# `P*V` on four 32-column tiles, shared scores behind the row sums: an attention and two-layer MoE kernel on one Trainium2 core

## The chip, the cores and the metric

The kernel runs on one core of a Trainium2 chip. The metric is the device time of one execution in microseconds (us). TensorE is called PE here, its weight loads PEld, VectorE DVE, ScalarE ACT, GpSimd POOL and SyncE SP, as in the profile.

## The reference

Attention with a soft cap over 2 batches of 12 heads, 448 rows, head size 64; its output feeds two feed-forward stages with gates.

```python
def _attn_ref(q, k, v, cap):
    scale = 1.0 / np.sqrt(q.shape[-1])
    scores = scale * np.matmul(q, k.transpose(0, 1, 3, 2))
    scores = cap * np.tanh(scores / cap)
    scores = scores - np.max(scores, axis=-1, keepdims=True)
    attn = np.exp(scores)
    attn = attn / (np.sum(attn, axis=-1, keepdims=True) + 1e-09)
    return np.matmul(attn, v)
...
def reference(**kwargs):
    ...
    x = np.ascontiguousarray(attn_out.transpose(0, 2, 1, 3)).reshape(B * S, H * D)
    x = _moe_ref(x=x, **moe_kwargs)      # h = x @ w_in; h * sigmoid(1.702 h) @ w_out
    return _moe2_ref(x=x, **moe2_kwargs) # rms norm, silu(x @ w_gate) * (x @ w_val) @ w_out
```

## The kernel before

The program has two parts, one behind the other: `attention()`, which works on the 24 heads as 12 pairs (p = 0 to 11), and `rest()`, the feed-forward stages, a long row of matrix products with weights that ACT and DVE decode on the way. The order of the work is written out by hand, in the loop over p at the end of `attention()`; each engine takes its instructions in the order in which this loop issues them. So an instruction that has to wait holds up all that stands behind it on its engine.

For a pair, PE turns q and k (`turn`, 64-row pieces), DVE splits them into a high and a low part (`split_kq`), and PE makes the transposed scores in four pieces of up to 128 keys: pieces 0 to 2 for both heads of the pair (`scores`, two 64-row tiles of the array side by side, into a two-bank tile `s`), and the last 64 keys of both heads together in one (`scores_last`, the full 128 x 128 array, into a one-bank tile `v`). These last are the shared scores. ACT takes tanh and exp of each piece (`exps`, tiles `tt` and, for the shared scores, `tl`). PE multiplies the result by v (`outputs`, `P*V`: the two heads on two 64-column tiles of the array side by side, in four rounds, one for each piece) and sums the rows (`sums`: four 32-column tiles side by side, in two rounds when DVE has added up the first three pieces, which it does for the pairs in `THIRD`, and in three for pairs 6 to 9). DVE copies `P*V` out (`zt`), takes the reciprocal of the sums, and POOL writes it to DRAM (`keep_recips`) and reads it back spread over all rows (`spread`, `r<-recs`); then come `norm_mul` (DVE), `norm_hi` (POOL, ACT for the last pairs) and `norm_lo` (DVE), which give the feed-forward part its x.

`P*V` and the sums of pair p-1 stand in the loop's pass p, behind the first scores of pair p+1. Tiles come from pools in PSUM: two buffers for `s` (`ps_s`), two for `v` (`ps_v`, which shared scores, `P*V` and sums share), one for `t`. A tile can be written only when what stood in its buffer has been read:

```python
ps_s = actx.enter_context(tc.tile_pool(name="ps_s", bufs=2, space=PSUM, reuse_waits="tile"))
ps_t = actx.enter_context(tc.tile_pool(name="ps_t", bufs=1, space=PSUM, reuse_waits="tile"))
ps_v = actx.enter_context(tc.tile_pool(name="ps_v", bufs=2, space=PSUM, reuse_waits="tile"))
```

Of the kernel before, what the change touches and what calls it, by code (L numbers as in the profile page):

```python
# [10 lines left out]
F32R = mybir.dt.float32r  # L11
# [7 lines left out]
def attn_moe_kernel(  # L19
# [14 lines left out]
    nc = tc.nc  # L34
# [8 lines left out]
    NC = 3  # L43
# [5 lines left out]
    def f(ap):  # L49
        return ap.bitcast(F32)  # L50
# [143 lines left out]
    def attention():  # L194
        with ExitStack() as actx:
# [14 lines left out]

            vns = [ap_.tile([128, 4, NC, D], F32, name=f"vn{i}", bufs=1) for i in range(3)]
            ves = [ap_.tile([128, 2, 2, D], F32, name=f"ve{i}", bufs=1) for i in range(3)]
            kbs = [ap_.tile([128, 2, 128], F32R, name=f"kb{i}", bufs=1) for i in range(2)]

            def constants():
                for kb in kbs:
# [71 lines left out]
            def split_kq(p):  # L288
                t = turned.pop(p)
                if p:  # L290
                    x = ap_.tile([128, 2, 2 * S], F32R, tag="x", name="x")
                    xs[p] = [[x[:, a, j * S:(j + 1) * S] for j in range(2)] for a in range(2)]
                    flat = t[:, :, 0:S].rearrange("p a (c n) -> p a c n", n=64)
                    high, low = [x[:, m].rearrange("p (c a n) -> p a c n", a=2, n=64) for m in range(2)]
                    nc.vector.tensor_copy(high, flat)
                    nc.vector.tensor_tensor(out=low, in0=flat, in1=f(high), op=ALU.subtract)  # L296
                    for e in range(2):
                        nc.gpsimd.tensor_copy(kbs[p % 2][half[e], :, half[e]], f(x[half[e], :, 384:S]))  # L298
                else:
                    ts = [t[1][:, 0:128], t[1][:, 128:S], t[0][:, 64:64 + S]]  # L300
                    xs[p] = [
                        [ap_.tile([128, w.shape[1]], F32R, name=f"x{a}{j}", bufs=1) for j, w in enumerate(ts)]
                        for a in range(2)
                    ]
                    for j in (2, 0, 1):
                        nc.scalar.activation(out=xs[p][0][j], in_=ts[j], func=AF.Copy)
                    for j in (2, 0, 1):
                        nc.vector.tensor_tensor(out=xs[p][1][j], in0=ts[j], in1=f(xs[p][0][j]), op=ALU.subtract)
                    for a in range(2):
                        for e in range(2):  # L310
                            nc.gpsimd.tensor_copy(kbs[0][half[e], a, half[e]], f(xs[p][a][1][half[e], 256:S - 128]))
# [16 lines left out]
            def scores_last(p):  # L328

                ps = ps_v.tile([128, 512], F32, tag="v", name="v")  # L330
                for n, (a, m) in enumerate(TERMS):
                    nc.tensor.matmul(  # L332
                        out=ps[:, 0:S], lhsT=kbs[p % 2][:, a], rhs=xs[p][m][-1], start=(n == 0), stop=(n == 2)
                    )
                return ps

            def exps(p, c, ps):
                if c == NC:
                    t = ap_.tile([128, S], F32, tag="tl", name="tl")
                    src_ = ps[:, 0:S]  # L340
                else:
                    t = ap_.tile([128, 2, S], F32, tag="tt", name="tt", bufs=8)
                    src_ = ps[:, :, 0:S]
                nc.scalar.activation(out=t, in_=src_, func=AF.Tanh, scale=tsc)  # L344
                nc.scalar.activation(out=t, in_=t, func=AF.Exp, scale=capt)  # L345
                pt[p, c] = t
# [4 lines left out]
            def outputs(p, cs=range(NC + 1)):  # L351

                g, i = place[p]
                if 0 in cs:
                    opened[p] = ps_v.tile([128, 512], F32, tag="v", name="v")
                ps = opened[p]
                for c in cs:
                    for e in range(2):
                        w = vns[g % 3][:, 2 * i + e, c] if c < NC else ves[g % 3][:, i, e]
                        nc.tensor.matmul(  # L360
                            out=ps[half[e], 0:S], lhsT=w, rhs=pt[p, c][:, e] if c < NC else pt[p, c],
                            start=(c == 0), stop=(c == NC), skip_group_check=True,
                        )
                if NC not in cs:
                    return
                zt[p] = zrp.tile([128, S], F32, tag="z", name="z", bufs=5)
                if p < NPR - 1:
                    nc.vector.tensor_copy(zt[p], ps[:, 0:S])
                else:
                    nc.scalar.activation(out=zt[p], in_=ps[:, 0:S], func=AF.Copy)  # L370
# [96 lines left out]
            def warm_up(times):  # L467
# [3 lines left out]
            warm_up(WARM)  # L471

            plan_a = {
                5: [(size, 0)], 7: [(size, 1)], 10: [(high_part, 0)],
                12: [(high_part, 1), (square, 2), (sign, 2), (mask, 2)], 13: [(square, 3), (sign, 3), (mask, 3)],
            }
            plan_d = {
                6: [(clip, 0), (field, 0)], 7: [(top, 0)], 8: [(low, 0)], 9: [(clip, 1), (field, 1)],
                10: [(top, 1), (low, 1)],
            }  # L480

            def decode(plan, p):
# [10 lines left out]
            turn(0)  # L493
            split_kq(0)
            s0 = scores(0, 0)
            for p in range(NPR + 1):
                if p < NPR:
                    exps(p, 0, s0)
                    if p != 1:
                        s1 = scores(p, 1)  # L500
                    exps(p, 1, s1)
                    s2 = scores(p, 2)
                    decode(plan_a, p)
                    exps(p, 2, s2)
                    last = scores_last(p)
                    exps(p, NC, last)
                    if p == 0:
                        turn(1)
                        split_kq(1)
                        outputs(0, range(2))  # L510
                        s0 = scores(1, 0)
                    if p + 2 < NPR:
                        turn(p + 2)
                        split_kq(p + 2)
                    for g, at_ in ((2, 0), (3, 0), (4, 1), (5, 3), (6, 5)):
                        if p == at_:
                            load_k(g)
                            load_q(g)
                    if p in (1, 2, 4, 5, 7):
                        load_v(2 + (1, 2, 4, 5, 7).index(p))  # L520
                    if p in (2, 4, 6):
                        load_to((2, 4, 6).index(p))
                    if 0 < p < NPR - 1:
                        s0 = scores(p + 1, 0)
                    if p == 0:
                        s1 = scores(1, 1)
                    if p != 1:
                        add_two(p)
                    if p == NPR - 2:
                        run(low_part, 0)  # L530
                else:
                    decode(plan_a, p)
                    run(low_part, 1)
                if p == 0:
                    outputs(0, range(2, NC + 1))
                elif p == 2:
                    outputs(1, range(2, NC + 1))
                elif p > 2:
                    outputs(p - 1)
                if 4 <= p < NPR:  # L540
                    norm_mul(p - 4)
                if p == NPR - 1:
                    both = ps_t.tile([128, 2, 512], F32, tag="t", name="late")
                    for n in range(2):
                        late[p - 2 + n] = both[:, :, n * SH:(n + 1) * SH]
                    spread_product(p - 2, [late[p - 2][:, j] for j in range(2)])
                if 3 <= p < NPR:
                    spread(p - 3)
                if p >= 1:
                    sums(p - 1)  # L550
                if 4 <= p < NPR:
                    norm_hi(p - 4)
                if 1 <= p < NPR - 2:
                    keep_recips(p - 1)
                if p == 1:
                    add_two(1)
                if p in THIRD:
                    add_third(p)
                if 4 <= p < NPR:
                    norm_lo(p - 4)  # L560
                if p == 1:
                    outputs(1, range(2))
                if p == NPR - 1:
                    normal(p - 2)
                if p == NPR:
                    spread_product(p - 2, [late[p - 2][:, j] for j in range(2)])
                    normal(p - 2, p - 4)
                    decode(plan_a, p + 1)
                decode(plan_d, p)
            return spread_product, norm_mul, norm_hi, norm_lo  # L570

    def rest(spread_product, norm_mul, norm_hi, norm_lo):
# [371 lines left out]
```

## Time and profile before

| | |
|---|---|
| timed runs | 603.66, 603.69, 604.91 us, median 603.69 |
| profiled execution | 607.85 us |
| its span, first to last instruction | 606.1 us |
| PE busy | 597.0 us (99% of the span) |
| ACT busy | 396.2 us (65%) |
| DVE busy | 454.0 us (75%) |

The attention part ends on PE at 107.31 us, where the first product of the feed-forward part starts. A matmul of this kernel is a group of records: an x12 row is twelve matmul records in sequence or side by side. Ends of matmuls are modelled, so lengths of PE's work are read from the start of one row to the start of the next.

### The profile page before, as it was taken

The page shows a single profiled execution, that of the slowest core. Times are in us where ns is not written, and L with a number is a line of the kernel's source. Part 1 is how long each engine was busy: PE and PEld are TensorE (multiplying, and loading weights), DVE is VectorE, ACT ScalarE, POOL GpSimd, SP SyncE. Part 2 cuts the span into 40 slices and gives each one's busy share as a digit, 9 for nine tenths or more (in the row PEclk, how much of TensorE's full clock was granted, in tenths as well). Part 3 has the DMA queues.
Part 4 walks back from the last instruction along what each step waited for, and adds up shares of the span by engine and source line. Part 5 has one row for each costly group of instructions (what it writes and reads, how often), then busy time and mean ns, then how long its engine had stood idle before and what let it go on. Part 6 is the DMA issues. An engine that isn't in the chain of part 4 may idle for free.

```text
span 606.1 us, 8596 instructions
## 1 busy us (share of the span) xinstructions
PE 597.0 (99%) x3389; PEld 506.4 (84%) x3389; DVE 454.0 (75%) x549; ACT 396.2 (65%) x532; POOL 76.9 (13%) x105
## 2 busy tenths in 40 slices
PE   8999899999999999999999999999999999999997
PEld 5455454889988899888888888899989999999997
DVE  2888799689874636667788899995588897588842
ACT  5999967789874547777676666674555483366400
POOL 4233441000000000000022203200022200122100
PEclk9999999999999999999999999999999999999999
DMA  6666422064453332333333333433233342233012
GB/s 152 157 182 170 127 76 91 1 184 135 152 157 104 105 104 73 120 122 105 104 105 107 101 105 107 136 123 104 62 120 122 114 132 86 97 104 105 0 79 104
DMA packets 78567, 67.16 MB, mean 111 GB/s; under 512 B 29440, under 2 KB 75830, under 8 KB 78528
## 3 DMA queue, kind: packets, MB, share of 16 engines
q1 hardware_dynamic: 74064, 64.27, 34.7%
q0 software_dynamic: 3664, 2.16, 1.2%
q8 instruction: 26, 0.43, 0.3%
q10 hardware_dynamic: 800, 0.20, 0.1%
q14 instruction: 13, 0.11, 0.1%
HBM read 63.80 MB, written 2.78 MB: 110 GB/s over the span
## 4 chain that ended last, share of the span: by engine, by line
PE 91%; DMA 3%; ACT 3%; DVE 2%; POOL 0%; issue 0%; POOLq 0%; DVEq 0%
PE b L630 22%; PE b L629 22%; PE b L628 22%; PE b L838 14%; PE v L360 4%; DMA r<-recs 3%; PE s L322 2%; PE v L393 1%; ACT tt L345 1%; ACT tt L344 1%; PE v L332 1%; PE v L469 1%; DVE rs L398 1%; POOL kb L298 0%; PE t L274 0%; DVE x L296 0%
## 5 line engine op out<-in xcount | busy, mean ns | idle before, releaser
L630 PE MATMUL b<-x,ring 128*128 128x512 f32 (+1 forms) x480 | 174.3, 363 | 0.0
L629 PE MATMUL b<-x,ring 128*128 128x512 f32 (+1 forms) x480 | 174.1, 363 | 0.0
L628 PE MATMUL b<-x,ring 128*128 128x512 f32 (+1 forms) x480 | 174.0, 362 | 0.0
L628 PEld LDWEIGHTS b<-x,ring 128*128 128x128 f32 x480 | 90.1, 188 | 10.4 <-issue 0.3
L629 PEld LDWEIGHTS b<-x,ring 128*128 128x128 f32 x480 | 90.1, 188 | 9.9
L630 PEld LDWEIGHTS b<-x,ring 128*128 128x128 f32 x480 | 90.1, 188 | 9.4
L838 PE MATMUL b<-ring,uA 128*128 128x384 f32 x504 | 87.8, 334 | 0.0
L838 PEld LDWEIGHTS b<-ring,uA 128*128 128x128 f32 x504 | 87.4, 188 | 0.0
L154 DVE SCALAR_TENSOR_TENSOR dec<-raw,dec 128x768 uint32<-128x768 uint32 x66 | 67.8, 1028 | 24.7 <-ACT dec L150 23.3
L160 DVE SCALAR_TENSOR_TENSOR dec<-raw,dec 128x768 uint32<-128x768 uint32 x68 | 73.2, 1077 | 1.1
L180 DVE TENSOR_TENSOR ring<-dec,ring 128x768 fp32r<-128x768 f32 x68 | 66.8, 984 | 4.7 <-ACT ring L175 4.6
L630 PE MATMUL b<-g,ring 128*128 128x384 f32 (+1 forms) x192 | 70.0, 365 | 0.0
L629 PE MATMUL b<-g,ring 128*128 128x384 f32 (+1 forms) x192 | 69.8, 364 | 0.0
L175 ACT ACTIVATE ring<-dec 128x768 fp32r<-128x768 f32 x68 | 56.7, 834 | 19.9 <-DVE dec L166 11.7
L628 PE MATMUL b<-g,ring 128*128 128x384 f32 (+1 forms) x192 | 69.6, 362 | 0.0
L166 DVE SCALAR_TENSOR_TENSOR dec<-raw,dec 128x768 uint32<-128x768 uint32 x68 | 65.0, 955 | 1.5
L146 ACT ACTIVATE dec<-dec,edge 128x768 f32<-128x768 f32 x66 | 61.6, 933 | 1.0
L142 ACT ACTIVATE dec<-raw 128x768 f32<-128x768 f32 x66 | 59.1, 896 | 0.8 <-DVE ring L180 0.5
L150 ACT ACTIVATE dec<-dec 128x768 f32<-128x768 f32 x66 | 55.6, 843 | 1.5
L806 POOL TENSOR_TENSOR a<-a,gg 128x512 f32<-128x512 f32 (+1 forms) x18 | 29.6, 1646 | 188.6 <-DVE gg L799 184.2
L809 ACT ACTIVATE uA<-a 128x512 fp32r<-128x512 f32 (+1 forms) x24 | 13.9, 579 | 46.3 <-POOL a L806 34.5
L730 POOL TENSOR_TENSOR sqs<-sqs,sq 128x384 f32<-128x384 f32 (+1 forms) x10 | 11.7, 1166 | 229.7 <-ACT sq L726 229.7
(107 smaller groups left out, 697.0 us busy)
## 6 DMA issues: line engine op xcount, KB each, us to landing
raw<-in_moe_w_out SPq DMA_DIRECT2D x20, 768.0 KB, 4.2
raw<-in_moe_w_in SPq DMA_DIRECT2D x16, 768.0 KB, 4.6
raw<-in_moe_w_gate SPq DMA_DIRECT2D x12, 768.0 KB, 4.2
raw<-in_moe_w_val SPq DMA_DIRECT2D x12, 768.0 KB, 4.3
raw<-in_moe_w_out SPq DMA_DIRECT2D x8, 512.0 KB, 3.7
out<-oacc SPq DMA_DIRECT2D x6, 384.0 KB, 2.3
raw<-in_moe_w_out SPq DMA_DIRECT2D x8, 256.0 KB, 3.4
r<-recs POOLq DMA_DIRECT2D x9, 224.0 KB, 7.7
```

The costliest lines, as they stand in the source:

```text
L142: nc.scalar.activation(out=f(d), in_=f(hi), func=AF.Square, scale=2.0 ** 15)
L146: nc.scalar.activation(out=f(d), in_=f(d), func=AF.Sign, bias=edge)
L150: nc.scalar.activation(out=f(d), in_=f(d), func=AF.Relu, scale=2.0 - 2.0 ** -23)
L154: nc.vector.scalar_tensor_tensor(out=d, in0=hi, scalar=3, in1=d, op0=ALU.logical_shift_left, op1=ALU.bitwise_and)
L160: nc.vector.scalar_tensor_tensor(out=d, in0=hi, scalar=0xC0000000, in1=d, op0=ALU.bitwise_and, op1=ALU.bitwise_or)
L166: nc.vector.scalar_tensor_tensor(out=d, in0=lo, scalar=29, in1=d, op0=ALU.logical_shift_right, op1=ALU.bitwise_or)
L175: nc.scalar.activation(out=t[:, 0], in_=f(dec_t[w][0]), func=AF.Copy)
L180: nc.vector.tensor_tensor(out=t[:, 1], in0=f(d), in1=f(t[:, 0]), op=ALU.subtract)
L628: nc.tensor.matmul(out=wide(o, b), lhsT=w0, rhs=x0, start=first, stop=False)
L629: nc.tensor.matmul(out=wide(o, b), lhsT=w0, rhs=x1, start=False, stop=False)
L630: nc.tensor.matmul(out=wide(o, b), lhsT=w1, rhs=x0, start=False, stop=last)
L838: nc.tensor.matmul(out=os_[t][n][:, 0:HW], lhsT=uA[xi][:, i, tok], rhs=w[:, wi, n * HW:(n + 1) * HW], start=(i == 0 and xi == 0 and wi == ...
```

## The change

Four things are changed. `P*V` of a pair runs on four 32-column tiles (two halves of each head) in place of two of 64 columns; the number of rounds stays four. The shared scores of pair p, and their tanh and exp, move from the front of pass p to behind the sums of pair p-1, except in the first and the last pass; for this `kb` and `x` get a third buffer, and the exps of the next pair's first piece go ahead of those of the shared scores. `spread` is issued at the front of POOL's part of a pass, ahead of the casts, and `norm_mul` stands behind the reciprocal, `norm_lo` a pass later. Two of the weight steps of the first units (`high_part`, `low_part` of unit 1) move into the last passes.

```diff
-            kbs = [ap_.tile([128, 2, 128], F32R, name=f"kb{i}", bufs=1) for i in range(2)]
+            kbs = [ap_.tile([128, 2, 128], F32R, name=f"kb{i}", bufs=1) for i in range(3)]
...
-                    x = ap_.tile([128, 2, 2 * S], F32R, tag="x", name="x")
+                    x = ap_.tile([128, 2, 2 * S], F32R, tag="x", name="x", bufs=3)
...
                 for c in cs:
-                    for e in range(2):
+                    for n in range(4):
+                        e, d0 = n // 2, n % 2 * 32
                         w = vns[g % 3][:, 2 * i + e, c] if c < NC else ves[g % 3][:, i, e]
                         nc.tensor.matmul(
-                            out=ps[half[e], 0:S], lhsT=w, rhs=pt[p, c][:, e] if c < NC else pt[p, c],
+                            out=ps[32 * n:32 * n + 32, 0:S], lhsT=w[:, d0:d0 + 32],
+                            rhs=pt[p, c][:, e] if c < NC else pt[p, c],
                             start=(c == 0), stop=(c == NC), skip_group_check=True,
                         )
...
-                5: [(size, 0)], 7: [(size, 1)], 10: [(high_part, 0)],
-                12: [(high_part, 1), (square, 2), (sign, 2), (mask, 2)], 13: [(square, 3), (sign, 3), (mask, 3)],
+                5: [(size, 0)], 7: [(size, 1)], 9: [(high_part, 0)], 11: [(high_part, 1)],
+                12: [(square, 2), (sign, 2), (mask, 2)], 13: [(square, 3), (sign, 3), (mask, 3)],
...
-                10: [(top, 1), (low, 1)],
+                10: [(top, 1), (low, 1)], 11: [(low_part, 1)],
...
+            exps(0, 0, s0)
             for p in range(NPR + 1):
+                early = p in (0, NPR - 1)
                 if p < NPR:
-                    exps(p, 0, s0)
                     if p != 1:
                         s1 = scores(p, 1)
                     exps(p, 1, s1)
                     s2 = scores(p, 2)
-                    decode(plan_a, p)
                     exps(p, 2, s2)
-                    last = scores_last(p)
-                    exps(p, NC, last)
+                    if early:
+                        last = scores_last(p)
+                        exps(p, NC, last)
+                        decode(plan_a, p)
+                    if p >= 3:
+                        spread(p - 3)
...
                     if 0 < p < NPR - 1:
                         s0 = scores(p + 1, 0)
+                    if p < NPR - 1:
+                        exps(p + 1, 0, s0)
...
+                    if p >= 5:
+                        norm_lo(p - 5)
...
                 elif p > 2:
                     outputs(p - 1)
-                if 4 <= p < NPR:
-                    norm_mul(p - 4)
+                if p in THIRD and p != 1:
+                    add_third(p)
+                if p < NPR - 2:
+                    decode(plan_d, p)
...
-                if 3 <= p < NPR:
-                    spread(p - 3)
                 if p >= 1:
                     sums(p - 1)
...
-                if p in THIRD:
-                    add_third(p)
...
                 if 4 <= p < NPR:
-                    norm_lo(p - 4)
+                    norm_mul(p - 4)
+                    norm_hi(p - 4)
+                if not early and p < NPR:
+                    last = scores_last(p)
+                    decode(plan_a, p)
+                    exps(p, NC, last)
```

On PE, before, in the pass of pair 3: two pieces of scores (`s_481`, `s_491`), the shared scores `v_501`, the transposes `t_508`, the next pair's first piece `s_536`, and `P*V` into `v_545`.

```order
L322 MATMUL s_481<-x_350 128x448 [waits PE_49]
L322 MATMUL s_481<-x_350 128x448 x5
L322 MATMUL s_491<-x_350 128x448 [waits Activation_49]
L322 MATMUL s_491<-x_350 128x448 x5
L332 MATMUL v_501<-x_350,kb1_111 128x448 [waits DVE_49,Pool_49]
L332 MATMUL v_501<-x_350,kb1_111 128x448 x2
L274 MATMUL t_508<-ident_58,kq1_103 128x64 x14
L322 MATMUL s_536<-x_439 128x448 [waits Activation_49]
L322 MATMUL s_536<-x_439 128x448 x5
L360 MATMUL v_545<-tt_394,vn1_105 64x448 [waits DVE_49]
```

The same place of the change, from the shared scores of pair 2 (`v_492`) to `P*V` of pair 2 (`v_561`):

```order
L332 MATMUL v_492<-x_281,kb2_112 128x448 [waits DVE_49,Pool_49]
L332 MATMUL v_492<-x_281,kb2_112 128x448 x2
L322 MATMUL s_499<-x_353 128x448 [waits Activation_49]
L322 MATMUL s_499<-x_353 128x448 x5
L322 MATMUL s_509<-x_353 128x448 [waits Activation_49]
L322 MATMUL s_509<-x_353 128x448 x5
L274 MATMUL t_521<-ident_58,kq1_103 128x64 x14
L322 MATMUL s_549<-x_446 128x448 [waits Activation_49]
L322 MATMUL s_549<-x_446 128x448 x5
L361 MATMUL v_561<-tt_376,vn1_105 32x448 x4
```

The shared scores are now the last thing of a pass, one pass's work ahead of the `P*V` that needs them (its fourth round reads `tl_496`); the first piece `s_549` takes the buffer that `s_499` had.

On ACT, in the change, the same stretch: what reads `s_456` (first piece of pair 3), `v_492` (shared scores of pair 2), then `s_499` and `s_509`.

```order
L344 ACTIVATE tt_463<-s_456,tsc_60 128x896 [waits PE_49]
L345 ACTIVATE tt_463<-tt_463,capt_59 128x896 [waits Activation_49]
L344 ACTIVATE tl_496<-v_492,tsc_60 128x448 [waits PE_49]
L345 ACTIVATE tl_496<-tl_496,capt_59 128x448 [waits Activation_49]
L344 ACTIVATE tt_506<-s_499,tsc_60 128x896 [waits DVE_49,PE_49]
L345 ACTIVATE tt_506<-tt_506,capt_59 128x896 [waits Activation_49]
```

Here the tanh of `s_499` (which frees the buffer for `s_549`) stands behind tanh and exp of the shared scores; before, it stood ahead of those of its own pair.

On POOL, one pass in the middle, before (casts for `kb`, the spread, `norm_hi`, the reciprocals to DRAM):

```order
L298 CAST kb0_110<-x_813 64x2x64 x2
L408 DMA r_841<-recs_662 128x1x448
L435 CAST x0_66<-z_554 128x448
L403 DMA recs_855<-rs_852 4x224
L298 CAST kb1_111<-x_907 64x2x64 x2
```

and in the change:

```order
L410 DMA r_832<-recs_691 128x1x448
L298 CAST kb2_112<-x_849 64x2x64 x2
L405 DMA recs_901<-rs_899 4x224
L437 CAST x0_66<-z_578 128x448
L410 DMA r_932<-recs_799 128x1x448
```

The spread now goes out right behind the `norm_hi` of the pass before, ahead of the casts, which wait for the split.

## Rows read from the trace of the kernel before

**Rows 1.** The page's first line.

```profile
span 606.1 us, 8596 instructions
```

**Rows 2.** Busy time of each engine in two stretches (columns as in the first line).

```profile
core 0: us, PE busy (x) PEld busy (x) DVE busy (x) ACT busy (x) POOL busy (x), PEclk, DMA share, GB/s
...
107.30:606.00 498.70, 495.35 (x2536) 453.26 (x2532) 369.94 (x451) 306.04 (x428) 41.28 (x28) 1.00 0.33 106
```

**Rows 3.** PE in order of time, one pair: start, length, operation, count.

```profile
41.67 2.48 PE L360 MATMUL v<-tt,vn 128*64 128x448 f32 x12
43.97 0.92 PE L360 MATMUL v<-tl,ve 128*64 128x448 f32 x4
44.82 0.59 PE L393 MATMUL v<-ts,ones 128*32 128x224 f32 x8
45.23 0.56 PE L393 MATMUL v<-tl,blk 128*32 128x224 f32 x8
45.72 1.49 PE L322 MATMUL s<-x 64*128 64x448 f32 x12
47.13 0.88 PE L332 MATMUL v<-x,kb 128*128 128x448 f32 x3
47.95 0.65 PE L274 MATMUL t<-ident,kq 64*128 64x64 f32 x14
48.40 0.85 PE L322 MATMUL s<-x 64*128 64x448 f32 x6
49.19 2.48 PE L360 MATMUL v<-tt,vn 128*64 128x448 f32 x12
```

**Rows 4.** ACT in order of time, one pair, and a weight step between pairs.

```profile
36.18 0.62 ACT L344 ACTIVATE tl<-v,tsc 128x448 f32<-128x448 f32 x1
36.83 0.67 ACT L345 ACTIVATE tl<-tl,capt 128x448 f32<-128x448 f32 x1
37.40 0.99 ACT L344 ACTIVATE tt<-s,tsc 128x896 f32<-128x896 f32 x1
...
43.32 0.61 ACT L344 ACTIVATE tl<-v,tsc 128x448 f32<-128x448 f32 x1
...
48.63 0.89 ACT L128 ACTIVATE dec<-raw 128x768 f32<-128x768 f32 x1
```

**Rows 5.** PE in order of time, `P*V` of pair 6; in brackets the wait ahead.

```profile
74.33 3.78 PE L360 MATMUL v<-tt,vn 128*64 128x448 f32 x12 [2.12 <-DVE rs L398]
77.88 1.37 PE L360 MATMUL v<-tl,ve 128*64 128x448 f32 x4
```

**Rows 6.** DVE in order of time, `norm_mul` ahead of that wait.

```profile
72.18 0.62 DVE L423 TENSOR_TENSOR z<-z,r 128x448 f32<-128x448 f32 x1 [3.18 <-DMA r<-recs]
```

**Rows 7.** What the view of line L408 (`spread`) says of its nine transfers.

```profile
DMA to landing us min/median/max: 6.8/7.7/10.4
```

**Rows 8.** Busy time and granted clock of two stretches behind that wait.

```profile
74.30:75.30 1.00, 0.97 (x6) 0.49 (x8) 1.00 (x2) 1.00 (x2) 0.55 (x1) 1.00 0.16 58
75.30:78.70 3.40, 3.40 (x13) 0.98 (x8) 3.37 (x4) 1.58 (x2) 0.82 (x1) 0.51 0.01 1
```

**Rows 9.** PE and ACT in order of time, where one waited for the other.

```profile
8.77 1.01 ACT L344 ACTIVATE tt<-s,tsc 128x896 f32<-128x896 f32 x1 [0.89 <-PE s L322]
9.83 0.88 PE L322 MATMUL s<-x,x 64*128 64x448 f32 x6 [0.50 <-ACT tt L344]
...
80.45 1.49 PE L322 MATMUL s<-x 64*128 64x448 f32 x12
81.37 1.01 ACT L344 ACTIVATE tt<-s,tsc 128x896 f32<-128x896 f32 x1 [4.46 <-PE s L322]
```

**Rows 10.** PE in order of time, row sums in three rounds (pair 8).

```profile
87.49 0.56 PE L393 MATMUL v<-tt,ones 128*32 128x224 f32 x8
87.87 0.56 PE L393 MATMUL v<-tl,blk 128*32 128x224 f32 x8
```

**Rows 11.** DVE and PE in order of time, first reciprocal and `P*V` of pair 1.

```profile
22.35 1.55 DVE L398 RECIPROCAL rs<-v 128x224 f32<-128x224 f32 x1
...
22.51 1.72 PE L360 MATMUL v<-tt,vn 128*64 128x448 f32 x8 [0.93 <-ACT tl L344]
```

More of the change, by code (lines that the diff above doesn't have):

```diff
@@ L297, in split_kq @@
                     for e in range(2):
-                        nc.gpsimd.tensor_copy(kbs[p % 2][half[e], :, half[e]], f(x[half[e], :, 384:S]))
+                        nc.gpsimd.tensor_copy(kbs[p % 3][half[e], :, half[e]], f(x[half[e], :, 384:S]))
                 else:
@@ L332, in scores_last @@
                     nc.tensor.matmul(
-                        out=ps[:, 0:S], lhsT=kbs[p % 2][:, a], rhs=xs[p][m][-1], start=(n == 0), stop=(n == 2)
+                        out=ps[:, 0:S], lhsT=kbs[p % 3][:, a], rhs=xs[p][m][-1], start=(n == 0), stop=(n == 2)
                     )
@@ L530, in attention @@
                         run(low_part, 0)
+                    if p >= 5:
+                        norm_lo(p - 5)
                 else:
                     decode(plan_a, p)
-                    run(low_part, 1)
+                    norm_lo(p - 5)
                 if p == 0:
@@ L546, in attention @@
                     spread_product(p - 2, [late[p - 2][:, j] for j in range(2)])
-                if 3 <= p < NPR:
-                    spread(p - 3)
                 if p >= 1:
                     sums(p - 1)
-                if 4 <= p < NPR:
-                    norm_hi(p - 4)
                 if 1 <= p < NPR - 2:
@@ L556, in attention @@
                     add_two(1)
-                if p in THIRD:
-                    add_third(p)
+                    add_third(1)
                 if 4 <= p < NPR:
-                    norm_lo(p - 4)
+                    norm_mul(p - 4)
[4 more added lines that the diff above has]
+                    exps(p, NC, last)
                 if p == 1:
                     outputs(1, range(2))
+                if NPR - 2 <= p < NPR:
+                    decode(plan_d, p)
                 if p == NPR - 1:
@@ L568, in attention @@
                     decode(plan_a, p + 1)
-                decode(plan_d, p)
             return spread_product, norm_mul, norm_hi, norm_lo
```

## The prediction, written before the changed kernel ran

> **What bounds the kernel now.** I read the busy times by stretch first. From 107.3 us on the feed-forward part takes 498.70 us of the span of 606.1, and PE works in 495.35 of it [rows 1, 2]: PE is the bound there, the change adds no work to it, and what the attention part gains or loses ahead of it goes to the end one for one. So I read PE's own order of time next. In the middle of the attention part one pair follows the next without a wait: from `P*V` at 41.67 to `P*V` at 49.19 are 7.52 us, all of it PE's work [rows 3]. The reader sees there `P*V` (2.30 for three rounds, 0.85 for the fourth), the sums (0.41 and 0.49), two pieces of scores (1.41), the shared scores (0.82), the transposes (0.45), the next first piece (0.79). ACT needs 7.14 for a pair (36.18 to 43.32) [rows 4], so it is nearly as full, 0.38 below PE.
>
> Then I looked for breaks. There is one that matters: ahead of `P*V` of pair 6 PE waited 2.12 us for the reciprocal, and then `P*V` took 3.78 and 1.37 [rows 5] where it takes 2.48 and 0.92 [rows 3]. The granted clock shows why: 0.51, the lower of its two levels (1.2 GHz in place of 2.4), in the 3.4 us from 75.3 on, after that wait [rows 8]. The wait begins on DVE: `norm_mul` stood 3.18 us for the spread reciprocals [rows 6], whose transfer needed 10.4 us, the longest of nine (median 7.7) [rows 7], and the reciprocal that PE needs stands behind it. Wait and low clock cost 2.12 + 1.75 = 3.87 us (1.75 is 3.78 + 1.37 less 2.48 + 0.92).
>
> **The spread and its use.** The transfer is now issued ahead of the casts, and its reader stands behind the reciprocal. Before, it had 10.4 - 3.18 = 7.2 us from issue to use. Now it goes out right behind the `norm_hi` of one pass and is read behind the reciprocal two passes later: two passes of 7.5 less reciprocal, `norm_mul`, cast and issue, some 3 us, leave about 12. The longest landing, 10.4, fits. So 3.87 us go; should a transfer be late all the same, it holds `norm_mul` and no longer the reciprocal. Term: -3.87, or 0 where the wait isn't there to begin with (below).
>
> **`P*V` on four tiles.** Rounds stay four, and a round has the same 448 columns. The sums show four 32-column tiles side by side: 0.38 for 224 columns (87.49 to 87.87) [rows 10], which is 0.76 for 448, against 0.77 for a round on two tiles of 64 (2.30 / 3) [rows 3]. So a round costs the same. What goes is the change of shape between `P*V` and sums: the fourth round takes 0.85 in place of 0.77, the first sum 0.41 in place of 0.38 [rows 3, 10], together 0.11 a pair.
>
> The Trainium skill ("TensorE: Matmul & The Clock Gate", section "Measured speedup vs the span model") speaks against such packing: it gives three column tiles side by side a speed-up of 2.38, which is 79% of three. By that, as an estimate, `P*V` would take 3.07 / 0.79 = 3.9 us a pair, 0.8 more, some 9 us for eleven pairs. The sums' rounds above, at 0.76 for 448 columns, don't show this loss.
>
> **The shared scores behind the sums.** This is the part that decides, and I think that it costs more than it gives. On PE alone it saves a shape change, about 0.1 a pair. But it closes a loop through ACT. The shared scores now end a pass; ACT takes their tanh and exp, and only then the tanh of the next pair's second piece; that one frees the buffer which the first piece of the pair after it needs (it waits for ACT in the order shown above); and behind that piece stand `P*V`, sums and the next shared scores. One turn of the loop:
> shared scores to ACT's start 0.92 (80.45 to 81.37, where ACT did wait for PE) [rows 9]; tanh 0.65 and exp 0.57 (36.18, 36.83, 37.40) [rows 4]; tanh of the second piece until PE goes on 1.06 (8.77 to 9.83, where PE did wait for ACT) [rows 9]; first piece 0.79; `P*V` 3.15 - 0.08 = 3.07; sums 0.38 + 0.49 = 0.87 [rows 3].
> Sum 7.93 us, where the pass took 7.52: +0.41. With a third round of sums both grow by 0.38 [rows 10]. A shape change from 32 columns to the full array stands nowhere in the trace; I take it as that from sums to scores, inside the 0.49. Bounds: without any handover above streaming the loop can't come below the 7.52 less 0.2 that PE itself needs; 8.1 if DVE's copy of `P*V`, which must now be done before the shared scores can take its buffer, comes 0.15 late.
> The loop holds in seven passes (from the second pieces of pair 4 to those of pair 11): 7 x 0.41 = 2.9. In the last of them the transposes (0.45) are missing; this shortens PE's own sum and not the loop: +0.4. Term: +3.3, from +1 to +4.5.
> ACT has 7.93 - 7.14 = 0.79 of room in a turn; the weight steps put ahead of the shared exps (0.89) [rows 4] overrun it once, in pass 5: +0.1. In passes 7 and 9 the third round of sums covers them.
>
> **The head.** The first reciprocal runs from 22.35 to 23.90, and DVE's order up to it is unchanged. `P*V` of pair 1 began at 22.51, when the tanh of its shared scores had freed a buffer [rows 11]. Now it takes the buffer of the sums, which this reciprocal reads: start 23.96. Behind it stand 1.7 of `P*V`, then scores and handover 0.92: ACT restarts at 26.6, takes three pieces of 1.97 ((7.14 - 1.22) / 3) until 32.5, and from the shared exps the loop runs on: + 7.93 - 0.92 to the shared scores of pair 3, + 0.82 to the next pieces, 40.3. Before they began at 45.72 - 7.52 = 38.2. Term: +2.1.
> PE waits here about 2 us, as long as the wait behind which the clock fell. There the fall came 1.0 us after work resumed [rows 5, 8]; here it would catch some 1.2 us of work on the path and cost as much. Bounds 0 and 1.2; I take 0.4, because a fall that comes a little later finds ACT at work and costs nothing.
>
> **The rest.** Two shape changes fewer at the end: -0.2. `norm_lo` a pass later, the third buffers and their memset lie beside PE's work. `high_part` and `low_part` of unit 1 leave the stretch behind the last exps, where ACT and DVE decode the next units while PE starts the feed-forward part; PE doesn't wait there now (495.35 busy, and its chain unbroken), and with less in front of them the later units come no later. Without that cover each 0.8 us of ACT would show.
>
> **Sum**, against the profiled 607.85 (span 606.1 and 1.75 around it): 2.1 + 3.3 + 0.1 + 0.4 - 3.87 - 0.2 = +1.8, so 609.7. The median of the timed runs, 603.69, is 4.16 below the profiled time; carried over, 605.5 us.
>
> **Rivals.**
> *The wait was never in the timed runs.* 4.16 is close to the 3.87 of wait and low clock; a transfer that lands 3 us earlier leaves neither. Two timed runs 0.03 apart speak for it, the third, 1.2 higher, for a wait that comes and goes. Then nothing is won back: 605.5 + 3.9 = 609.4. Chance 0.26.
> *The loop doesn't bind* (the faster side). If the handovers through ACT were 0.41 shorter in all, PE would run on its own work, 7.52 - 0.2: seven passes give -1.5, and with +2.1, -3.87 and -0.2 the time is 600.2. It decides from a loop of 7.52 down. Against it: of 0.92 and 1.06 about 0.57 and 0.99 are streaming itself, so all of what is left would have to vanish. Chance 0.15.
> *A loop somewhat short.* 7.85 in place of 7.93, no fall of the clock and a head of +1.8: 605.5 - 0.6 - 0.4 - 0.3 = 604.2, not to be told from before. Chance 0.27.
> *The four tiles share a path.* If they ran two by two, a round would take twice 0.77: +3 us a pair, over 630 us. The sums speak against it. Chance 0.02; this is the mechanism of the skill's 2.38 above, in its extreme.
>
> **How the numbers follow.** The sum as it stands has 0.30: 605.5 us, and with the other cases the range is 602.2 to 609.2, which leaves out most of the faster rival and the upper part of the first. About 0.2%, 1.2 us, is what a measurement of this kernel can tell from no change. Slower: 0.30 + 0.26 + 0.02 = 0.58. Same: 0.27. Faster: 0.15.
>
> **What would show it.** Right: in every middle pass a wait of PE of about 0.6 us ahead of the first piece (`scores`), released by ACT's tanh; a pass of 7.9 and 8.3 us; ACT waiting up to 0.8 for the shared scores; no wait of the reciprocal for the transfer; a wait of some 2 us for DVE's reciprocal ahead of `P*V` of pair 1; rounds of `P*V` at 0.76. Wrong: passes of 7.3 without a wait; or rounds above 0.8; or waits for decoded weights behind 108 us, which the sum leaves out.

## The result, and the profile after

The changed kernel takes 608.33 us (median of 6 runs, 608.11 to 610.46), the kernel before, beside it, 604.13 us (6 runs, 603.66 to 604.91). The ratio is 1.0078, with a 95% interval from 1.0065 to 1.0090: slower by 0.8%, which is 4.7 us (the medians lie 4.2 apart). That lies inside the forecast range and on the forecast side, but 2.8 us above the 605.5 given as likeliest. It is near the first rival's 609.4, that the wait had never been in the timed runs.

The profiled executions alone would say something else: 608.16 us after against 607.85 before, nearly the same. So the first question is which of the two is a typical execution. Of the changed kernel, the page's first line, two stretches of busy time with the granted clock (PEclk), and PE in order of time: `P*V` of pair 1, then one pair of the middle.

```profile
span 606.4 us, 8970 instructions
```

```profile
23.20:27.50 4.30, 4.24 (x48) 2.53 (x48) 2.62 (x3) 2.86 (x4) 0.62 (x1) 1.00 0.85 192
...
107.96:606.40 498.44, 495.01 (x2536) 453.07 (x2532) 369.64 (x451) 305.50 (x427) 41.35 (x28) 1.00 0.33 106
```

```profile
23.19 1.71 PE L361 MATMUL v<-tt,vn 128*32 128x448 f32 x16 [1.82 <-DVE rs L400]
...
38.83 0.85 PE L332 MATMUL v<-x,kb 128*128 128x448 f32 x3
39.61 1.49 PE L322 MATMUL s<-x 64*128 64x448 f32 x12
40.93 0.59 PE L274 MATMUL t<-ident,kq 64*128 64x64 f32 x14
42.00 0.87 PE L322 MATMUL s<-x 64*128 64x448 f32 x6 [0.47 <-ACT tt L344]
42.80 2.46 PE L361 MATMUL v<-tt,vn 128*32 128x448 f32 x24
45.08 0.94 PE L361 MATMUL v<-tl,ve 128*32 128x448 f32 x8
45.83 0.56 PE L395 MATMUL v<-ts,ones 128*32 128x224 f32 x8
46.21 0.56 PE L395 MATMUL v<-tl,blk 128*32 128x224 f32 x8
46.85 0.85 PE L332 MATMUL v<-x,kb 128*128 128x448 f32 x3
...
70.68 0.56 PE L395 MATMUL v<-tl,blk 128*32 128x224 f32 x8
71.17 0.87 PE L332 MATMUL v<-x,kb 128*128 128x448 f32 x3
```

From shared scores to shared scores a pass now takes 46.85 - 38.83 = 8.02 us, where it took 7.52 [rows 3], and PE stands still in it, ahead of the first piece of the next pair, for ACT's tanh. In the whole attention part such waits sum up to 4.8 us in nine places, 0.47 in most; the one of 0.50 right behind the first scores stands before the change too [rows 9], so 4.3 us in eight places are new. ACT and DVE in the same pass, in order of time, and the first reciprocal:

```profile
39.72 0.64 ACT L344 ACTIVATE tl<-v,tsc 128x448 f32<-128x448 f32 x1 [0.81 <-PE v L332]
40.38 0.67 ACT L345 ACTIVATE tl<-tl,capt 128x448 f32<-128x448 f32 x1
40.96 0.99 ACT L344 ACTIVATE tt<-s,tsc 128x896 f32<-128x896 f32 x1
```

```profile
21.59 1.55 DVE L400 RECIPROCAL rs<-v 128x224 f32<-128x224 f32 x1
...
46.08 0.62 DVE L370 COPY z<-v 128x448 f32<-128x448 f32 x1 [1.23 <-PE v L361]
```

The reader sees the ring close: PE waits for ACT's tanh of 40.96, that stands behind the exps of the shared scores, and ACT had waited 0.81 for PE's shared scores of 38.83. Neither engine is full (7.46 of 8.02 us for PE), and both wait in each pass. Of transfers of the reciprocals nothing is waited for; the view of `spread`'s line (L410) says

```profile
DMA to landing us min/median/max: 6.8/8.1/9.4
```

### The profile page after: what moved, and what is told of

It reads as the page before. It is cut to its first block, busy times and chain, and to the rows that moved or that the text cites. A ratio compares the mean times of both kernels' runs of the same rounds, so it can differ in the third digit from the quotient of the medians.

```text
span 606.4 us, 8970 instructions
## 1 busy us (share of the span) xinstructions
PE 592.8 (98%) x3581; PEld 506.1 (83%) x3581; DVE 454.7 (75%) x549; ACT 396.8 (65%) x532; POOL 79.8 (13%) x106
## 3 DMA queue, kind: packets, MB, share of 16 engines
q0 software_dynamic: 3664, 2.16, 1.3%
## 4 chain that ended last, share of the span: by engine, by line
PE 92%; ACT 4%; DVE 2%; issue 1%; DMA 1%; SPq 0%
PE b L643 22%; PE b L642 22%; PE b L641 22%; PE b L851 14%; PE v L361 5%; ACT tt L344 2%; PE s L322 2%; PE v L395 1%; PE v L332 1%; ACT tl L344 1%; ACT tt L345 1%; DVE x L296 1%; DVE x L295 1%; DMA kq<-in_k 1%; ACT tl L345 0%
## 5 line engine op out<-in xcount | busy, mean ns | idle before, releaser
L641 PEld LDWEIGHTS b<-x,ring 128*128 128x128 f32 x480 | 90.1, 188 | 10.4 <-issue 0.3
```

Of the source, the lines that this page charges most:

```text
L641: nc.tensor.matmul(out=wide(o, b), lhsT=w0, rhs=x0, start=first, stop=False)
```

## The experiments

My theory after the result: the wait of before belongs to single executions, so nothing was won back; late head and loop through ACT are the whole loss. Rivals: the wait is in the timed runs too and the change loses some 8 us elsewhere; or the four tiles or DVE set the longer pass.

The last column is the attention part in the profiled execution, from PE's first scores to the first product of the feed-forward part (both starts in brackets). It leaves out the start of the program, which varies by itself (last section).

| kernel | median us | ratio to before, 95% | attention us |
|---|---|---|---|
| before, profile shown ahead | 603.69 | | 99.71 (7.60, 107.31) |
| changed | 608.33 | 1.0078, 1.0065 to 1.0090 | 101.17 (6.79, 107.96) |
| b_again | 603.60 | 1.0000, 0.9992 to 1.0009 | 95.87 (6.85, 102.72) |
| spread_only | 603.94 | 1.0003, 0.9994 to 1.0012 | 96.62 (6.84, 103.46) |
| four_only | 603.70 | 1.0002, 0.9992 to 1.0012 | 96.69 (7.76, 104.45) |
| early_all | 602.64 | 0.9976, 0.9965 to 0.9986 | 94.97 (7.45, 102.42) |
| head_only | 606.68 | 1.0054, 1.0042 to 1.0067 | 99.68 (7.59, 107.27) |
| exp_later | 605.23 | 1.0033, 1.0022 to 1.0044 | 98.07 (6.76, 104.83) |
| exp_later_head | 603.72 | 1.0002, 0.9993 to 1.0012 | 96.44 (7.44, 103.88) |
| pad_loop | 614.68 | 1.0185, 1.0167 to 1.0204 | 106.66 (6.75, 113.41) |

The first four experiments ran beside 35 runs of before (median 603.93), the last four beside 17 (603.22); they are compared by their ratios.

**b_again: before once more, unchanged.**

> The kernel before, unchanged, for a second profile and more times. Theory A (the wait for the late reciprocals belongs to the one profiled execution and not to the timed ones): no wait of PE ahead of P*V of pair 6, no stretch at the lower clock in the attention part, feed-forward part about 3.9 us earlier than 107.31, so about 103.4, span about 602.2, time 603.7 to 604.2. Theory B (every execution has it, and the timed ones are shorter elsewhere): again a wait of about 2 us and the lower clock behind it, span about 606.

The page's first line, PE at the `P*V` that had waited, and the line on `spread`'s transfers. (The texts ahead call it that of pair 6. It is pair 7's: the sums behind it are the second with three rounds, and pairs 6 to 9 have three.)

```profile
span 601.5 us, 8596 instructions
```

```profile
70.65 0.86 PE L322 MATMUL s<-x 64*128 64x448 f32 x6
71.44 2.48 PE L360 MATMUL v<-tt,vn 128*64 128x448 f32 x12
73.74 0.92 PE L360 MATMUL v<-tl,ve 128*64 128x448 f32 x4
```

```profile
DMA to landing us min/median/max: 6.8/7.4/9.1
```

No wait, and `P*V` takes 2.30 and 0.85 (starts 71.44, 73.74, sums at 74.59). Where [rows 5] show 2.12 of waiting and [rows 8] the lower clock, there is nothing; the longest landing is 9.1 in place of 10.4 [rows 7]. The attention part is 3.84 us shorter, which is the 3.87 of the prediction. Theory A holds: the profile that the prediction was read from was a rare execution: at 607.85 it lies above all 35 timed runs of before in this comparison, the highest of which took 605.76. The granted clock says the same: its mean over the span was 0.997 in that execution, and 0.999 or 1.000 in each of these 35, in the ten of b_again and in the 17 beside the later experiments.

**spread_only: the moves around `spread` alone, on the kernel before.**

```diff
                     exps(p, NC, last)
+                    if p >= 3:
+                        spread(p - 3)
...
-                if 4 <= p < NPR:
-                    norm_mul(p - 4)
...
-                if 3 <= p < NPR:
-                    spread(p - 3)
                 if p >= 1:
                     sums(p - 1)
...
+                if 4 <= p < NPR:
+                    norm_mul(p - 4)
+                    norm_hi(p - 4)
```

(`norm_lo` goes a pass later, as in the change.)

> The kernel before with nothing but the moves around the spread: issued ahead of the casts, used behind the reciprocal, norm_lo a pass later. Theory A (the timed runs of before have no such wait): within 0.5 us of before. Theory B (the wait is in them): 3 to 4 us faster.

Ratio 1.0003: nothing was won in the median. Its runs lie closer together, 603.56 to 604.40, against 603.09 to 605.76 of before. The profile has no wait for a transfer, but one new wait of PE, for DVE's copy of `P*V`, which DVE now reaches later near the end:

```profile
98.88 2.48 PE L360 MATMUL v<-tt,vn 128*64 128x448 f32 x12 [0.69 <-DVE z L368]
```

**four_only: `P*V` on four tiles alone, on the kernel before** (the change's edit of `outputs`, nothing else).

> The kernel before with nothing but P*V on four 32-column tiles. By the sums' rounds a round stays at 0.75 to 0.77 and two shape changes a pair cost 0.11 less, where PE is the bound: eleven pairs, -0.4 to -1.2 us, because ACT needs 7.14 of a pass and some handovers come up where PE gets ahead. By the rule that side-by-side column tiles lose a fifth: a round of 0.95, about +9 us.

Ratio 1.0002, so the expected gain did not come. PE in order of time, and the longest waits of PE and of DVE (total, times, longest):

```profile
65.94 2.46 PE L361 MATMUL v<-tt,vn 128*32 128x448 f32 x24 [1.51 <-DVE rs L400]
68.22 0.94 PE L361 MATMUL v<-tl,ve 128*32 128x448 f32 x8
```

```profile
PE v L361 <- DVE rs L400: 2.1, 2, 1.5
...
DVE z L425 <- DMA r<-recs: 4.3, 3, 2.0
```

The tiles do what they were costed at: a round takes 2.28 / 3 = 0.76, and the attention part is 96.69, of which 2.05 (0.54 + 1.51) are waits for the reciprocal; without them 94.64, 1.2 below b_again's 95.87. But PE gets to the reciprocal earlier, and the transfer that DVE waits for comes no sooner: in this execution the gain turns into this wait. It is not a typical one: it took 605.18, where the twelve runs reach from 602.53 to 605.24 with a median of 603.70. What the runs near the median wait for is not shown. The lowest, 602.53, lies 0.56 below the lowest of before, 603.09.

The Trainium skill ("TensorE: Matmul & The Clock Gate", section "Measured speedup vs the span model") measured a speed-up of 2.38 for three column tiles side by side. If that loss of a fifth against three held here, a round would take, as an estimate from this figure, 0.76 / 0.79 = 0.96; these rows show 0.76. That section of the Trainium skill states its figure for 32-column tiles with 512 columns moving, as a gain of packing; four such tiles against two of 64 it does not compare.

**early_all: the changed kernel with all shared scores back at the front of the pass.**

```diff
-                early = p in (0, NPR - 1)
+                early = True
```

> The changed kernel with the shared scores and their exps back ahead of the transposes in every pass; four tiles and the moves of the spread stay. Theory A (loop through ACT and late head are the whole loss): no wait of 0.47 ahead of the first piece, passes of 7.35 to 7.5, P*V of pair 1 about 1.4 us earlier, 4.5 to 5.5 us faster than the changed kernel, so 602.8 to 603.8, 0.3 to 1.3 us below before. Rival (four tiles or the later use of the reciprocals lose the time): no better than 606.5.

```profile
22.36 1.71 PE L361 MATMUL v<-tt,vn 128*32 128x448 f32 x16 [0.95 <-ACT tl L344]
...
40.12 0.65 PE L274 MATMUL t<-ident,kq 64*128 64x64 f32 x14
40.58 0.85 PE L322 MATMUL s<-x 64*128 64x448 f32 x6
41.36 2.46 PE L361 MATMUL v<-tt,vn 128*32 128x448 f32 x24
...
48.73 1.71 PE L361 MATMUL v<-tt,vn 128*32 128x448 f32 x16
```

No wait in the middle passes, a pass of 48.73 - 41.36 = 7.37, and `P*V` of pair 1 is 14.91 behind the first scores, where the changed kernel needs 16.40. 602.64 us, ratio 0.9976: this beats both kernels, before by 0.24% (0.14 to 0.35). So the four tiles and the earlier spread are not what loses, and the shared scores' place is. Each of the two gave nothing by itself; together in this kernel they do, which fits the reading that in four_only the wait for the transfer took what the tiles gave, but does not show it: this kernel also has the third buffers, the earlier exps and the moved weight steps, which weren't tried apart.

**head_only: the shared scores of pair 1 alone back.**

```diff
-                early = p in (0, NPR - 1)
+                early = p in (0, 1, NPR - 1)
```

> The changed kernel with the shared scores of pair 1 alone back ahead of the sums, so that P*V of pair 1 takes the other buffer. Theory A (the head is a loss of its own, passed on by the loop): P*V of pair 1 starts about 1.4 us earlier and all that follows with it; 1.3 to 2.1 us faster than the changed kernel, 606.2 to 607.0; the passes stay at 8.02 with the wait of 0.47. Rival (the loop has slack behind the head and takes it up): no change, 608.3.

```profile
22.50 1.71 PE L361 MATMUL v<-tt,vn 128*32 128x448 f32 x16 [0.95 <-ACT tl L344]
...
41.32 0.87 PE L322 MATMUL s<-x 64*128 64x448 f32 x6 [0.47 <-ACT tt L344]
42.12 2.46 PE L361 MATMUL v<-tt,vn 128*32 128x448 f32 x24
...
50.14 2.46 PE L361 MATMUL v<-tt,vn 128*32 128x448 f32 x24
```

1.0054 in place of 1.0078, 1.4 us, and 1.49 in the attention part. The pass stays at 8.02 (42.12 to 50.14): the loop neither takes up nor adds to what the head lost.

**exp_later: 0.57 us out of the loop.**

```diff
                 nc.scalar.activation(out=t, in_=src_, func=AF.Tanh, scale=tsc)
-                nc.scalar.activation(out=t, in_=t, func=AF.Exp, scale=capt)
+                if c == 1 and p > 1:
+                    nc.scalar.activation(out=pt[p - 1, NC], in_=pt[p - 1, NC], func=AF.Exp, scale=capt)
+                if c < NC or p in (0, NPR - 1):
+                    nc.scalar.activation(out=t, in_=t, func=AF.Exp, scale=capt)
```

> The changed kernel with one instruction of ACT moved: the exp of the shared scores behind the tanh of the next pair's second piece, which takes 0.57 out of the loop and leaves ACT's work and PE's order as they are. Theory A (the loop through ACT sets the pass): the pass falls from 8.02 to about 7.5, by 0.5 and not by 0.57, because the second piece's own handover, 0.92 + 1.06 against 1.95 of PE's work beside it, comes up; passes with a weight step gain less; 1.5 to 3 us faster, 605.3 to 606.8. Rival (PE's own order or DVE's copy sets the pass): 608.3, pass 8.02.

ACT in order of time:

```profile
46.98 0.64 ACT L344 ACTIVATE tl<-v,tsc 128x448 f32<-128x448 f32 x1 [0.34 <-PE v L332]
47.81 1.01 ACT L344 ACTIVATE tt<-s,tsc 128x896 f32<-128x896 f32 x1 [0.19 <-PE s L322]
48.72 0.66 ACT L346 ACTIVATE tl<-tl,capt 128x448 f32<-128x448 f32 x1
```

and PE, from `P*V` to `P*V`:

```profile
42.05 2.46 PE L364 MATMUL v<-tt,vn 128*32 128x448 f32 x24
...
48.87 0.87 PE L322 MATMUL s<-x 64*128 64x448 f32 x6
49.67 2.46 PE L364 MATMUL v<-tt,vn 128*32 128x448 f32 x24
```

The same work in another order of one instruction: 1.0033, 2.7 us less, 3.10 less in the attention part. The pass is 7.62 (`P*V` at 42.05 and 49.67), 0.40 less, a little less than expected. ACT now waits 0.19 for the second piece as well, and PE's next first piece starts 1.06 behind that tanh (47.81 to 48.87): read from these rows, the second piece's own handover is the next ring. No run tried it.

**exp_later_head: both repairs** (exp_later's edit for the pairs from 2 on, and head_only's).

> The changed kernel with both repairs, the shared scores of pair 1 ahead of the sums and the later exp. If the two losses add up, 608.3 less 1.3 to 2.1 less 1.5 to 3: 603.2 to 605.5, about as before; still above the version with all shared scores at their old place, 602.6, because the second piece's handover stays uncovered. If one contains the other: no better than the better of the two by itself.

1.0002, and 96.44 in the attention part: 4.73 below the changed kernel, where the two repairs by themselves gave 1.49 and 3.10, in sum 4.59. They add up, and are two losses. It is as fast as before and no faster.

**pad_loop: one instruction more in the loop, whose result nobody reads.**

```diff
                 nc.scalar.activation(out=t, in_=src_, func=AF.Tanh, scale=tsc)
+                if c == NC and 0 < p < NPR - 1:
+                    pad = ap_.tile([128, S], F32, tag="pad", name="pad", bufs=1)
+                    nc.scalar.activation(out=pad, in_=t, func=AF.Copy)
```

> The changed kernel with one more instruction of ACT in the middle passes, a copy of 128x448 between tanh and exp of the shared scores, whose result nobody reads; 0.5 to 0.6 us of ACT, which waits 0.8 in a pass for the shared scores. Theory A (the loop sets the pass): the slack does not help, since the copy lies inside the loop: passes of 8.5 to 8.6, ten passes, 4.5 to 5.5 us slower, 612.8 to 613.8. Rival (ACT has 0.8 of room): not slower than 608.8.

```profile
48.91 0.64 ACT L344 ACTIVATE tl<-v,tsc 128x448 f32<-128x448 f32 x1 [0.77 <-PE v L332]
49.58 0.58 ACT L347 ACTIVATE pad<-tl 128x448 f32<-128x448 f32 x1
50.19 0.67 ACT L348 ACTIVATE tl<-tl,capt 128x448 f32<-128x448 f32 x1
```

```profile
43.98 2.46 PE L364 MATMUL v<-tt,vn 128*32 128x448 f32 x24
...
52.61 2.46 PE L364 MATMUL v<-tt,vn 128*32 128x448 f32 x24
```

ACT still waits 0.77 in the pass, although it got 0.61 more to do (49.58 to 50.19), and `P*V` follows `P*V` by 8.63 (43.98 to 52.61): all of it went into the pass. The attention part is 5.49 longer. The timed median, 614.68, is 0.9 above what I expected. Its four runs lie in two pairs: 613.58 and 613.62, inside the expected range, with a mean granted clock of 1.000, and 615.75 and 616.03 with one of 0.997. So the lower clock stands beside the extra time; where it fell is not known, as the profiled execution is of the first pair. A wait on an engine is no room on it if it waits for the ring.

## Why the prediction was right and where it was wrong

It was right on the side and, but for one step, near on the sizes; the step that failed is the -3.87 of the sum carried over to the median ("carried over, 605.5 us"). The profiled execution did have the wait and the lower clock, and the change does remove them, but the runs that the median is made of did not have them (b_again). The profiled time of 607.85 and the median of 603.69 stood 4.16 apart, nearly the stall itself; the prediction saw that, priced it as a rival at 609.4 and gave it 0.26. It should have been the main case: a profiled time above all three timed runs, and above their median by about the size of the largest irregular wait in its trace and what followed it. That 608.33 lies inside the stated range is in part luck: the case that came, at 609.4, lay above the range's end of 609.2, and came out lower because two terms were too high, the 0.4 for the clock and the 0 for the feed-forward part.

The other terms, each by the starts of rows, against the trace of b_again. The head ends with the second pieces of pair 4, the loop with those of pair 11, the tail with the first product of the feed-forward part. The rows at these places that are not shown above, of the changed kernel and then of b_again:

```profile
96.81 1.49 PE L322 MATMUL s<-x 64*128 64x448 f32 x12
```

```profile
37.51 1.49 PE L322 MATMUL s<-x 64*128 64x448 f32 x12
...
91.32 1.49 PE L322 MATMUL s<-x 64*128 64x448 f32 x12
```

| term | forecast | measured |
|---|---|---|
| head, to the second pieces of pair 4 | +2.1 | +2.16 (32.82 against 30.66 behind the first scores) |
| lower clock behind the head's wait | +0.4 | 0 |
| loop, seven passes, and weight steps | +3.3 and +0.1 | +3.39 (57.20 against 53.81) |
| tail | -0.2 | -0.25 (11.15 against 11.40) |
| feed-forward part | 0 | -0.34 (498.44 against 498.78) |
| stall | -3.87 | 0 |

The measured terms sum up to +4.96 us; the timed runs give 4.7.

- Head: `P*V` of pair 1 waits 1.82 for the reciprocal and starts 1.45 later, by the first scores. head_only shows that 1.49 hang on this one place. The rest is read from the rows: 8.33 for 8.11 from there to the second pieces of pair 3 (23.19 to 31.52; in b_again 21.80 to 29.91), with a wait of 0.68 for DVE's copy ahead of the shared scores at 30.76, and 8.09 for 7.60 on to those of pair 4, with the first wait for ACT's tanh (0.51). The prediction had this last turn of the loop in its head, and not the wait for the copy.
- Clock: granted 1.00 from 23.2 to 27.5, behind that wait. In the profile the term falls away (the last section has four longer runs at a lower mean clock).
- Feed-forward part: the 0.34 came with the moves around `spread`, for spread_only has it too (span 601.9, first product at 103.46: 498.44). Why these shorten it was not looked for.
- Loop, the size of the turn: 0.89 from shared scores to ACT, 0.66 and 0.58 of tanh and exp, 1.04 of the second piece's tanh, 0.80, 3.03, and 1.02 from the sums to the shared scores make 8.02; forecast was 7.93. The sums are the part that is off, 1.02 for 0.87. DVE's copy ends at 46.08 + 0.62 = 46.70, and the shared scores, which take its buffer, start 0.15 later. In the passes with a third round (0.49 from the last sum to the shared scores, 70.68 to 71.17) it is not seen. That was named as the upper bound, 8.1. This is read from the rows; the copy itself was not moved. A pass with three rounds took 8.28 (71.97 to 80.25), forecast 8.31.
- That the ring is the cause is shown from both sides: 0.57 out of it gives 0.40 a pass (exp_later), 0.61 into it costs 0.61 (pad_loop), and without it the pass is 7.37 (early_all). "The loop doesn't bind" is refuted.
- Weight step: the pass that holds one took 8.05 (55.65 to 63.70), 0.03 more, forecast 0.1. ACT starts on the shared scores 0.89 behind PE there too (54.87 to 55.76), right behind the step, so the step fills ACT's wait and adds nothing; ACT's waiting does cover work that lies outside the ring.
- `P*V`: rounds of 0.76 as read from the sums. The gain of 1.2 is there in four_only's trace if its waits are taken off; in the changed kernel it lies inside the ring's turn. The last rival calls a shared path the mechanism of the 2.38. The Trainium skill ("TensorE: Matmul & The Clock Gate", section "Measured speedup vs the span model") names no such mechanism for it. The rounds of 0.76 show no shared path here.
- Spread: no wait of DVE for the transfers, as said; in the median there was little to remove.
- Nothing waits for decoded weights behind 108 us, as the prediction assumed; PE is busy 495.01 of 498.44.

## What to carry to other kernels

Before an irregular wait in a trace goes into a sum, compare the profiled time with the timed runs: if it stands out by about that wait, cost the change against the runs without it, or profile once more. When work moves behind another step, follow its result through every engine back to the step that has to wait for it: a ring of handovers can be longer than any engine's own work, it shows as two engines that wait for each other in each pass, and here work taken out of the ring shortened the pass, while work put into it where an engine waited lengthened it in full. A faster step can run into a transfer that comes no sooner, as in the profile of four_only, and that profile stands out from its timed runs as well. The version that kept the four tiles and the earlier spread and left the shared scores in place was the fastest, 602.64 us.

## What the runs showed of the hardware that was not expected

- The clock fell to 0.51 behind one wait of 2.12 us in the middle of the attention part [rows 5, 8] and stayed at 1.00 behind one of 1.82 (changed kernel, 23.2 to 27.5) and one of 1.51 (four_only, from 66.0 to 70.2).
- Four timed runs that were not profiled show a mean granted clock of 0.996 or 0.997 and stand 2.1 to 2.4 us above the median of the others of their kernel: 610.46 of the changed kernel, 607.34 of exp_later, 615.75 and 616.03 of pad_loop. All three kernels have the late head, with its wait of 1.82; of the 16 runs of head_only and exp_later_head, which don't, none shows less than 0.999, nor does any of the 62 of before in the experiments. That fits a fall of the clock behind the late head in some executions; no profile shows it.
- The start varies between executions of one kernel: the first scores of before begin at 7.60 in one profile and at 6.85 in the other. Eight transposes ahead of them start at 5.30 and 5.35 and take 1.59 (to 6.89) in the first and 0.89 (to 6.24) in the second, with a granted clock of 1.00 in both. In the ten profiles it lies at 6.8 or at 7.4 to 7.8. Why, stays open; it is up to 1.0 us between two single executions (6.75 and 7.76).
- The transfer of the spread reciprocals, the same bytes nine times in each kernel, took from 6.7 to 10.6 us to land.
